# One-hots of the token ranks moved from VectorE to GpSimd, and their table products put one turn later

## The chip, the core and the metric

The kernel runs on one core of one Trainium2 chip. The metric is the device time of one launch in microseconds (us). The runs of the kernel before took 353.4, 355.7 and 352.9 us, a median of 353.4 us. One further execution was recorded by the hardware profiler; its own time is given below beside its span.

## What is computed

The reference first runs a gated linear attention over 4 batches, 8 heads, 768 positions and 48 features, with a complex decay for each feature. Then it sends each of the 3072 resulting rows to one of 8 experts.

```python
mag = np.sqrt(a_re * a_re + a_im * a_im)
scale = np.minimum(mag, 0.999) / (mag + 1e-06)
for t in range(S):
    S_re, S_im = (ar * S_re - ai * S_im + kv, ar * S_im + ai * S_re)
    y[:, :, t] = np.einsum('bhd,bhde->bhe', q[:, :, t], S_re)
...
logits = x @ w_gate + modality_bias[modality_id]
e_idx = np.argmax(logits, axis=1)
...
for e in range(E):
    h = np.maximum(x[mask] @ w1[e], 0.0)
    out[mask] = gate_w[mask, None] * (h @ w2[e])
```

## The kernel before, in words

**The attention part.** The 768 positions are cut into 6 chunks of 128; with 4 batches that makes 24 columns of 128 tokens. `gate_loop` walks over them in turns `w` from -4 to 24. Several stages are in flight in a turn: the decays of columns some turns ahead (angles `u`, waves `css`, moduli `pm`), the scaled queries and keys (`hats`, lines L276 and L280, which write `qkp` and `QK`), their transposes (`turned`, L304: `tKT` and `tQT`), the products within a column (`inner`: `wp` L321, the masked `W` L322, `up` L329, then `mid` L334, `U` L339, `state` L341), the output (`outer`: `yp` L353 and L359), and the rows with the logits (`rows`: `xw` L370, a copy `xr` L373 that is stored to `x_rows`, and the sum `lg` L374 on VectorE). Even turns also make the log sums `ls` L240, odd turns the angles `u` L194 and L195.

**The router.** `Router.take(m0, m1, ...)` is a generator that handles a group of columns in steps, one step for each turn. Four groups are taken: columns 0 to 8 from turn 8 on, 8 to 16 from turn 16 on, 16 to 20 from turn 20 on, and 20 to 24 after the last turn (`takes`). The first step picks each token's expert on VectorE. The second step counts, by products with a triangle of ones on TensorE, which rank a token has in its expert (`rank`), splits that position into its low 7 bits and the rest (`part` L654), and makes two one-hot matrices for each column: `lo` (128 tokens by 128, L658, the one-hot times the token's number) and `hi` (128 tokens by 194, L660, the one-hot times a power of two for the column), both bf16. The third step multiplies them on TensorE into a table (`table` L665), adds it to `so_far` on VectorE (L672), and after column 16 also runs `early_places` (some 30 small VectorE instructions from `counted` L688 to L690 on) and makes the index list `rows`, from which the first tokens can be gathered. Between its first and second step, gate weights `gw` (L619, L621) are worked out and stored to `x_rows` by small transfers on SyncE's queue (L624).

**The experts.** `Layers` loads two guessed experts' weights on GpSimd's queue (`w1` L863, `w2` L872) while the turns still run, issues gathers of token rows on GpSimd's queue (L913) from turn 22 on, once the first `rows` and `column` are there, transposes them (`xg_ps` L933), and runs two products per tile (`h_ps` L951, `y_ps` L966), whose results GpSimd's queue scatters (L971).

**What sets the order.** The Tile framework plans the order of each engine's instructions ahead of time, from the order of the program text, from when an instruction's inputs are there by its own costs, and from when a buffer comes free. On the chip each engine then goes through its list in that order. PSUM results share four slots (`pair`, tag "pair", bufs=4): `tKT`, `tQT`, `ls`, `wp`, `up`, `yp`, `xw`, `u`, `rank`, `cnt` and `table` take them in turn, and each waits until the reader of the one four places earlier is done. `lo` and `hi` have eight buffers each, `part` two. SyncE's queue (loads of `V` L285 and of q and k L138 and L139, stores of `x_rows`) and GpSimd's queue go in order too. [...]

Of the kernel before, what the change touches and what calls it, by code (L numbers as in the profile page):

```python
# [14 lines left out]
Alu = mybir.AluOpType  # L15
# [475 lines left out]
class Router:  # L491
# [88 lines left out]
    def take(self, m0, m1, late, dense):  # L580

        nc, rp, TP, E = self.nc, self.rp, self.TP, self.E
        n = m1 - m0
        last = m1 == len(self.tile_of)
# [68 lines left out]
        part = rp.tile([TP, 2, M], F32, name="part")  # L653
        nc.vector.tensor_copy(part[:, :, 0:n], part_i[:, :, 0:n])  # L654
        made = []
        for i in range(n):
            lo = rp.tile([TP, 128], BF16, name="lo", bufs=8)
            nc.vector.tensor_scalar(lo[:], self.iob[:, 0:128], part[:, 0, i:i + 1], self.p1[:], Alu.is_equal, Alu.mult)  # L658
            hi = rp.tile([TP, self.NC], BF16, name="hi", bufs=8)
            nc.vector.tensor_scalar(hi[:], self.iob[:, 0:self.NC], part[:, 1, i:i + 1], 2.0 ** self.tile_of[m0 + i], Alu.is_equal, Alu.mult)  # L660
            made.append((lo, hi))
        yield
        table = self.bank([128, self.NC], "table")
        for i, (lo, hi) in enumerate(made):
# [421 lines left out]
```

## Time and profile before

| | us |
|---|---|
| median of the runs | 353.4 |
| profiled execution, own time | 343.76 |
| its span in the trace | 341.9 |
| TensorE busy | 301.9 |
| VectorE busy | 256.0 |
| ScalarE busy | 241.2 |
| GpSimd busy | 70.0 |

The span is the time from the first to the last instruction of the trace. Busy time is the sum over instructions of an engine, overlaps counted once. On VectorE neighbouring instructions overlap by a little, so the distance between two starts says more about the cost of an instruction than its duration does. A bracket behind a row gives the idle time of the engine ahead of the instruction and what ended it. TensorE's attention turns lie between some 30 and 250 us; the experts' tiles follow until the end.

### The profile page before, as it was taken

Reading aid. Unit: us, or ns where it says so; the run is one execution under the profiler, and the core shown is the slowest. Engines: PE = TensorE matmul, PEld = TensorE weight load, DVE = VectorE, ACT = ScalarE, POOL = GpSimd, SP = SyncE. Lnnn points to the kernel's source line nnn. Section 1 sums busy time; section 2 is a strip of 40 time slices with the busy share of each in tenths; the row PEclk is TensorE's granted clock in tenths of the full one; section 3 lists DMA queues with packets and bytes.
Section 4 is the critical chain, followed back from the end, with each engine's and each line's share of the span. In section 5 each row is a group of like instructions: output and inputs, shape, how many; then the busy total and the mean of one; then the engine's idle time right before and its main releaser. Section 6 shows DMA issues by size and latency. Waiting matters only on the chain.

```text
span 341.9 us, 11679 instructions
## 1 busy us (share of the span) xinstructions
PE 301.9 (88%) x4982; PEld 232.8 (68%) x4982; DVE 256.0 (75%) x514; ACT 241.2 (71%) x301; POOL 70.0 (20%) x89
## 2 busy tenths in 40 slices
PE   1785999799989998999989999989999999979960
PEld 0342677577876878777777878789877687756740
DVE  2659799999895989999898889985679356543420
ACT  3888899999993999888898986445236554533530
POOL 8000000000000000001000001014202787887740
PEclk9999899899976999999999999999999999998995
DMA  7968788796777287864979794565110232322320
GB/s 144 219 117 164 154 182 161 115 188 136 134 179 131 63 141 168 148 142 67 160 176 181 149 166 80 86 87 117 39 38 18 81 111 83 104 92 92 113 90 4
DMA packets 158306, 41.21 MB, mean 121 GB/s; under 512 B 149107, under 2 KB 154632, under 8 KB 158250
## 3 DMA queue, kind: packets, MB, share of 16 engines
q1 hardware_dynamic: 152570, 30.08, 45.2%
q0 software_dynamic: 5680, 10.34, 12.5%
q8 instruction: 41, 0.67, 0.8%
q14 instruction: 15, 0.12, 0.1%
HBM read 36.39 MB, written 7.35 MB: 128 GB/s over the span
## 4 chain that ended last, share of the span: by engine, by line
PE 37%; ACT 21%; DVE 18%; DMA 9%; issue 8%; POOL 2%; SPq 2%; ACTq 0%; POOLq 0%; DVEq 0%
PE y_ps L966 6%; PE h_ps L951 6%; ACT sq L119 4%; PE up L329 4%; ACT L116 4%; PE yp L359 3%; PE xw L370 3%; PE u L194 3%; ACT css L119 3%; DMA qk<-in_k_dram 3%; DMA xg<-x_rows,idx 2%; PE wp L321 2%; ACT pm L119 2%; DMA abs<-in_a_re_dram 2%; DVE qkp L276 2%
## 5 line engine op out<-in xcount | busy, mean ns | idle before, releaser
L280 DVE TENSOR_TENSOR QK<-css,qkp 128x1536 f32<-128x1536 f32 x24 | 42.0, 1751 | 0.2
L329 PE MATMUL up<-V,QK 64*96 64x48 f32 x704 | 37.6, 248 | 2.4 <-DVE lg L374 2.4
L329 PEld LDWEIGHTS up<-V,QK 64*96 64x96 f32 x704 | 34.5, 162 | 4.2 <-DVE lg L374 2.8
L966 PE MATMUL y_ps<-w2t,hT 128*128 128x384 bf16 x200 | 36.8, 337 | 0.3 <-ACT hT L954 0.3
L971 POOL DMA_INDIRECT out_dram<-y_sb,idx x25 | 30.4, 1217 | 32.0 <-ACT y_sb L969 24.7
L863 POOL DMA_DIRECT2D abs<-in_moe_w_dram x2 | 1.8, 906 | 168.9 <-ACT sq L119 168.9
L951 PE MATMUL h_ps<-xgT,w1t 128*128 128x256 bf16 (+1 forms) x312 | 34.9, 268 | 0.0
L116 ACT ACT_TABLE_LOAD x25 | 32.1, 1283 | 1.4 <-PEq L1070 0.9
L951 PEld LDWEIGHTS <-w1t 128*128 128x128 bf16 x312 | 29.5, 98 | 4.6
L913 POOL DMA_INDIRECT xg<-x_rows,idx x25 | 28.8, 1153 | 14.5 <-issue 9.4
L305 ACT COPY KT<-tKT 96x1024 f32<-96x1024 f32 x24 | 24.2, 1006 | 10.2 <-PE tKT L304 10.2
L969 ACT ACTIVATE y_sb<-y_ps,xg 128x384 f32<-128x384 f32 x25 | 13.2, 577 | 24.8 <-PE y_ps L966 23.2
L321 PEld LDWEIGHTS wp<-QT,KT 96*64 96x64 f32 x768 | 24.3, 138 | 9.1 <-ACT yT L360 2.7
L321 PE MATMUL wp<-QT,KT 96*64 96x64 f32 x768 | 27.6, 225 | 2.9 <-ACT yT L360 2.0
L966 PEld LDWEIGHTS <-hT 128*128 128x128 bf16 x200 | 19.4, 101 | 13.5 <-issue 2.4
L370 PE MATMUL xw<-sel,yT 64*128 64x56 f32 x384 | 27.1, 283 | 0.7 <-ACT QT L305 0.7
L360 ACT COPY yT<-yp 128x512 f32<-128x512 f32 x24 | 14.0, 583 | 19.3 <-PE yp L359 19.2
L370 PEld LDWEIGHTS xw<-sel,yT 64*128 64x128 f32 x384 | 24.0, 193 | 2.6 <-ACT QT L305 0.8
L956 DVE TENSOR_SCALAR hT<-h_ps 128x1024 bf16<-128x1024 f32 (+1 forms) x10 | 11.7, 1171 | 18.4 <-PE h_ps L951 18.4
L194 PE MATMUL u<-tan,turn 128*128 128x384 f32 x48 | 23.3, 570 | 2.1 <-ACT tan L119 2.1
L305 ACT COPY QT<-tQT 96x1024 f32<-96x1024 f32 x24 | 24.3, 1013 | 0.8 <-PE tQT L304 0.7
L119 ACT ACTIVATE sq<-sq 128x1536 f32<-128x1536 f32 (+1 forms) x20 | 23.3, 1165 | 1.5 <-DVE sq L150 1.3
(209 smaller groups left out, 626.7 us busy)
## 6 DMA issues: line engine op xcount, KB each, us to landing
abs<-in_a_re_dram SPq DMA_DIRECT2D x24, 192.0 KB
abs<-in_a_im_dram SPq DMA_DIRECT2D x24, 192.0 KB
qk<-in_q_dram SPq DMA_DIRECT2D x24, 192.0 KB
qk<-in_k_dram SPq DMA_DIRECT2D x24, 192.0 KB
V<-in_v_dram SPq DMA_DIRECT2D x24, 192.0 KB
cb<-f_scr SPq DMA_DIRECT2D x10, 384.0 KB
x_rows<-xr SPq DMA_DIRECT2D x24, 96.0 KB
abs<-in_moe_w_dram POOLq DMA_DIRECT2D x2, 768.0 KB, 8.4
```

What stands on the lines that cost most here:

```text
L116: then(nc.scalar.preload_act_table_set(name))
L119: then(nc.scalar.activation(*args, **kw))
L194: nc.tensor.matmul(us[:, i], turn[:], tan[:, i], start=True, stop=False)
L280: nc.vector.tensor_tensor(QK[:].rearrange("p a h c d -> p a (h c d)"), wave, twice, Alu.mult)
L305: nc.scalar.copy(to[:], tp)
L321: nc.tensor.matmul(wp[rows_, h, :], KT[:, s, h], QT[:, s, h], start=True, stop=True)
L329: ins = nc.tensor.matmul(up[:, s, h], flat[rows_, h * C:(h + 1) * C], V[rows_, h, 0:D], start=True, stop=True)
L370: ins = nc.tensor.matmul(xw[:, u, j], yT[at_u, j], sel[at_u, j], start=True, stop=True)
L913: got = nc.gpsimd.indirect_dma_start(out=xg, out_offset=None, in_=self.x_rows, in_offset=bass.IndirectOffsetOnAxis(ap=idx[:, s, 0:1], axis=0))
L951: nc.tensor.matmul(h_ps[:, f // nf, f % nf, :], w1t[:, k, ff * 128:(ff + 1) * 128], xgT[:, k, :], start=(k == 0), stop=(k == KD - 1))
L966: nc.tensor.matmul(y_both[:, s], self.hT[:, f, s * 128:(s + 1) * 128], w2t[:, f, :], start=(f == 0), stop=(f == NF - 1))
L971: sc = nc.gpsimd.indirect_dma_start(out=self.out, out_offset=bass.IndirectOffsetOnAxis(ap=idx[:, s, 1:2], axis=0), in_=y_sb[:], in_offset= ...
```

## The change

In `Router.take`, the one-hots of the first three groups (20 columns, 40 instructions) go to GpSimd; the last group stays on VectorE. For the first three groups the generator also yields once more between the one-hots and the table products, so that the products and what follows them (`so_far`, and after column 16 `early_places` and the first `rows`) come in the turn after.

```diff
         made = []
         for i in range(n):
             lo = rp.tile([TP, 128], BF16, name="lo", bufs=8)
-            nc.vector.tensor_scalar(lo[:], self.iob[:, 0:128], part[:, 0, i:i + 1], self.p1[:], Alu.is_equal, Alu.mult)
+            eng = nc.vector if last else nc.gpsimd
+            eng.tensor_scalar(lo[:], self.iob[:, 0:128], part[:, 0, i:i + 1], self.p1[:], Alu.is_equal, Alu.mult)
             hi = rp.tile([TP, self.NC], BF16, name="hi", bufs=8)
-            nc.vector.tensor_scalar(hi[:], self.iob[:, 0:self.NC], part[:, 1, i:i + 1], 2.0 ** self.tile_of[m0 + i], Alu.is_equal, Alu.mult)
+            eng.tensor_scalar(hi[:], self.iob[:, 0:self.NC], part[:, 1, i:i + 1], 2.0 ** self.tile_of[m0 + i], Alu.is_equal, Alu.mult)
             made.append((lo, hi))
+        if not last:
+            yield
         yield
         table = self.bank([128, self.NC], "table")
```

## The prediction

> **What bounds the kernel now.** I read the page's busy times first, then the windows view for the turns in which the one-hots are made, then the chain of waits that ended last, then what TensorE waited for, and at last the instructions of each engine in order of time.
>
> ```profile
> PE 301.9 (88%) x4982; PEld 232.8 (68%) x4982; DVE 256.0 (75%) x514; ACT 241.2 (71%) x301; POOL 70.0 (20%) x89
> ```
> ```profile
> 142.40:151.50 9.10, 8.55 (x184) 6.96 (x184) 9.10 (x42) 7.24 (x9) 0.00 (x0) 1.00 0.74 166
> 151.50:160.00 8.50, 7.26 (x185) 6.59 (x185) 8.50 (x16) 8.10 (x10) 0.49 (x1) 1.00 0.13 17
> 212.00:230.00 18.00, 16.84 (x398) 14.67 (x398) 17.63 (x72) 8.20 (x12) 0.88 (x1) 1.00 0.61 88
> 230.00:236.00 6.00, 6.00 (x160) 5.67 (x160) 1.45 (x3) 3.50 (x8) 3.95 (x4) 1.00 0.84 155
> 242.00:248.00 6.00, 6.00 (x139) 5.41 (x137) 5.54 (x20) 0.82 (x2) 0.00 (x0) 1.00 0.14 38
> ```
>
> Behind the length of each window stand the busy times of TensorE, of its weight loads, of VectorE, ScalarE and GpSimd, then the clock granted to TensorE, the DMA share and GB/s. The averages of the page hide two states. Where the first two groups of one-hots are made (142 to 160 and 212 to 230 us), VectorE is full: 9.10 of 9.10, 8.50 of 8.50, 17.63 of 18.00. TensorE is nearly full beside it: 8.55, 7.26, 16.84. Where the third group is made (242 to 248), TensorE is full, 6.00 of 6.00. GpSimd does next to nothing in all of them. So there are two limits close together, and what VectorE is relieved of is worth only as much as TensorE stands still for VectorE.
>
> The chain of waits does run through the one-hots (start, us, what):
>
> ```profile
> 147.52 0.23 DVE lo L658
> ...
> 159.04 0.58 SPq L138
> 159.63 0.05 issue
> 159.68 9.29 DMA qk<-in_k_dram
> ```
>
> Read alone, this says that the one-hots lie on the path that sets the end. But the chain is one path of several that are about as long. The view of the waits of TensorE between 147 and 228 us (total, times, longest) says what it lost there:
>
> ```profile
> PE tQT L304 <- DVE eci L690: 1.2, 1, 1.2
> PE up L329 <- DVE lg L374: 1.0, 1, 1.0
> PE wp L321 <- DVE lg L374: 0.9, 1, 0.9
> PE wp L321 <- ACT yT L360: 0.7, 2, 0.4
> PE ls L240 <- DVE lg L374: 0.6, 1, 0.6
> PE tKT L304 <- DVE gw L621: 0.3, 1, 0.3
> ```
>
> The five on VectorE (DVE) make 4.0 us in 81. One of them, the 1.0 of `up`, I put down to the transfer of q and k (9.29 us in the chain), for which VectorE waits at that place. The other four, 1.2 + 0.9 + 0.6 + 0.3 = 3.0 us, are what TensorE loses to a VectorE that is late behind the one-hots.
>
> **The change part by part.**
>
> *VectorE is relieved.* Its rows around the first group (start, us):
>
> ```profile
> 147.45 0.30 DVE L658 TENSOR_SCALAR lo<-iob,part,p 128x128 bf16<-128x128 bf16 x1
> ...
> 150.43 0.29 DVE L658 TENSOR_SCALAR lo<-iob,part,p 128x128 bf16<-128x128 bf16 x1
> 150.65 0.26 DVE L660 TENSOR_SCALAR hi<-iob,part 128x194 bf16<-128x194 bf16 x1
> 150.83 0.67 DVE L322 TENSOR_TENSOR W<-wp,mask 128x512 f32<-128x512 f32 x1
> ```
>
> The durations, 0.29 and 0.26, would make 20 x 0.55 = 11 us. They overlap, though: eight pairs stand between 147.45 and the start of `W` at 150.83, so they cost 3.38 us, and one pair 0.42. Twenty pairs free 8.4 us of VectorE. What TensorE can make of it is at most the 3.0 us above; the third group gives nothing, since TensorE never waits there. SyncE's queue does not widen this: its load of q and k is issued at 159.04, behind TensorE's products of that turn in the chain, so it comes earlier only by what TensorE gains. Bounds of this gain: 0 and 3.0 us.
>
> *GpSimd is loaded.* No GpSimd row shows this instruction. The nearest are these three, one from the view of each source line (count, then min/median/max in ns):
>
> ```profile
> L48 POOL TENSOR_SCALAR_AFFINE_SELECT mask<-mask x1: 291/291/291, 2.6 to 2.6; 128x128 f32<-128x128 f32 x1
> L54 POOL TENSOR_SCALAR half<-mask x1: 544/544/544, 3.7 to 3.7; 128x128 f32<-128x128 f32 x1
> L559 POOL TENSOR_SCALAR_AFFINE_SELECT tri<-ones x1: 778/778/778, 7.6 to 7.6; 128x128 bf16<-128x128 bf16 x1
> ```
>
> The tensor-scalar of 128 elements takes 0.54 us; `hi` has 194, so scaled it is 0.82, and a pair 1.36. The low end is the select `mask` (0.29 and 0.44, a pair 0.73), the high end the bf16 select `tri` (0.78 and 1.18, a pair 1.96). I take 1.36, since it is the same kind of instruction. Eight pairs are 10.9 us (5.8 to 15.7), four pairs 5.4 us. The positions `part` are there at about 147 (the first `lo`), 214 and 243.8:
>
> ```profile
> 213.78 0.18 DVE part L654
> ```
> ```profile
> 243.58 0.17 DVE L654 CAST part<-part_i 128x8 f32<-128x8 int32 x1
> ```
>
> So undisturbed one-hots end at about 158, 225 and 249.2.
>
> *The products wait for them.* One turn later, they stand behind the angles `u` of the odd turn or behind its rows `xw`:
>
> ```profile
> 161.48 0.33 PE L195 MATMUL u<-neg,halfb 128*128 128x384 bf16 x1
> ```
> ```profile
> 227.95 1.10 PE L370 MATMUL xw<-sel,yT 64*128 64x56 f32 x16
> ...
> 249.70 2.00 PE L370 MATMUL xw<-sel,yT 64*128 64x56 f32 x32
> ```
>
> That is at 161.8 for the first group, at 229.0 for the second, and about 250.7, between the two halves of the last `xw` rows, for the third. The covers are 3.8, 4 and 1.5 us, less what TensorE gains: enough at 1.36 us a pair. At 1.96 a pair the one-hots end at 162.7, 229.7 and 251.6, so TensorE would wait 0.9 + 0.7 + 0.9 = 2.5 us. That is the price if the cover goes.
>
> *The two engines share something.* This speaks against the change, and the trace shows it at its start, where both run:
>
> ```profile
> 6.53 0.83 DVE L159 TENSOR_SCALAR neg<-abs 128x768 bf16<-128x768 f32 x1 [5.41 <-DMA abs<-in_a_re_dram]
> 7.29 0.94 DVE L157 TENSOR_TENSOR tan<-abs 128x768 f32<-128x768 f32 x1
> ```
> ```profile
> L159 DVE TENSOR_SCALAR neg<-abs x12: 544/550/835, 6.5 to 165.5; 128x768 bf16<-128x768 f32 x12
> ```
>
> The `neg` at 6.53 takes 0.83 us beside a working GpSimd, against a median of 0.55, so 0.28 more. The select `tri` on GpSimd (7.6 to 8.4) lies under VectorE's two-input `tan` (7.29 to 8.23) and takes 0.78; `mask`, made while VectorE is idle, takes 0.29, so 0.49 less. If every one of sixteen GpSimd instructions met a VectorE instruction in this way, VectorE would lose 16 x 0.28 = 4.5 us, more than the 3.38 it is spared, and GpSimd 16 x 0.49 = 7.8 us. The other end is no loss at all. Part of VectorE's work in these turns reads PSUM (`W`, `mid`, `U`), and neither row was taken with such work; I take six tenths, nearer to the two rows than to nothing. VectorE loses 2.7 of the 3.38 us, and GpSimd ends 4.7 us later for the big groups and, with less work beside it, some 1.2 us later for the small one: at about 162.6, 229.6 and 250.4. VectorE's net relief is then 0.7 us a group, so TensorE gains some 0.5 us at each of the first two groups (-1.0). It waits 0.8 and 0.6 us for the first two products, and 0.2 us more at each because it arrives earlier (+1.8).
>
> [...]
>
> *What else moves.* The load of w1 stands behind the first one-hots on GpSimd's queue, and the gathers near the third group's:
>
> ```profile
> 159.51 1.02 POOL L863 DMA_DIRECT2D abs<-in_moe_w_dram  x1 [151.13 <-ACT sq L119]
> ...
> 230.58 1.06 POOL L913 DMA_INDIRECT xg<-x_rows,idx  x1 [3.55 <-ACT idx L908]
> ```
>
> If the one-hots end at 162.6, w1 starts 3 us later than 159.51; what hides it are the turns up to 250, before whose end no product reads it. `early_places` and the first `rows` go one turn, some 6 us, later. VectorE has room there (1.45 busy of 6.00 from 230 on), so nothing is added; without that room it would be their some 30 small instructions. The first gather goes from 230.58 to about 237; six of them at 1.06 us and a gap end near 245, and their first use is a transpose behind the last `xw`, after 251.7 (249.70 and 2.00): hidden by 3 us and more after landing. They do share GpSimd's queue with the third group (5.4 us from 243.8 on) and can push its end from 250.4 to about 251.7, which costs 0 to 1.0 us of TensorE; I take 0.7. The `table` takes its PSUM slot one turn later. The wait of 1.2 us for `eci` is such a slot wait, on a small read that stands late in VectorE's list. It may go or come back double: -1.2 to +1.2, taken as 0, as neither row nor order tells.
>
> **Sum.** -1.0 + 1.8 + 0.7 + 0 = +1.5 us. Against the profiled execution's own 343.8 us that is 345.3. The runs shown have a median of 353.4, 9.6 us more than this one execution; I carry the difference over: 354.9 us, 0.4% more.
>
> **The rivals.**
>
> *GpSimd is starved, and TensorE waits for the products (slower).* The two-input instructions are the bulk of VectorE's turns (mean in ns behind the busy time):
>
> ```profile
> L280 DVE TENSOR_TENSOR QK<-css,qkp 128x1536 f32<-128x1536 f32 x24 | 42.0, 1751 | 0.2
> L276 DVE TENSOR_TENSOR qkp<-qk,pm 128x768 f32<-128x768 f32 x24 | 22.7, 948 | 1.0 <-DMA qk<-in_k_dram 0.9
> ```
>
> Two of each come in two turns, 2 x 1.75 + 2 x 0.95 = 5.4 us, and with a `tan` and a `sq` of 0.94 each 7.3 us. If GpSimd stands still during all of them, the first group ends at 147 + 10.9 + 7.3 = 165.2, 3.4 us behind the place of its product; the second, with 5.4 us beside it, at 214 + 10.9 + 5.4 = 230.3, 1.3 us behind. With 1.1 us lost net by VectorE at each big group (4.5 against 3.38) and 1.3 us at the third group, that is 3.4 + 1.3 + 2.2 + 1.3 = +8.2: 361.6 us, 2.3% more. It makes the kernel slower by over 1% as soon as the waits for the products exceed some 4 us together, that is from about 1.7 us a pair with 0.3 us lost by VectorE for each instruction. For it: VectorE is busy 8.50 of 8.50. Against it: some of its work reads PSUM, and the planner can put other products ahead.
>
> *VectorE's relief comes through whole (faster).* GpSimd goes undisturbed and all four waits go: -3.0, so 350.4 us, 0.8% less. To be faster by over 1% the wait of 1.0 at `up` must go too: 349.4 us. The 8.4 us of VectorE cannot come back, as TensorE is full.
>
> *The relief was hidden anyway.* TensorE's waits only change places, and GpSimd is in time: 353.4 us.
>
> **How the numbers follow.** About 1% (3.5 us) is what a measurement of this kernel can tell from no change. My sum (0.30), the case of no effect (0.12) and the faster case where it stays at -3.0 (0.08) make "within 1%" 0.50. The starved GpSimd, from over 1% on, has 0.40; faster by over 1% has 0.10. The range runs from 350.4, all four waits gone, to 361.6, the starved case in full; about one in ten lies outside at either side. The likeliest case alone has 351.9 to 356.9.
>
> **What would show it.** Right: one-hots on GpSimd at 1.3 to 2 us a pair; `QK`, `qkp` or `sq` beside them longer than 1.75 and 0.95; the waits of 0.9, 0.6 and 0.3 smaller; table products that wait about 1 us; the first gather near 237. Wrong: table products with waits of several us or one-hots of over 2 us a pair (the starved case); VectorE's instructions unstretched and none of the four waits left (the faster one). A new order of the planner, with waits at places not named here, would make the whole working miss.

## The result, and the profile after

| | before | after |
|---|---|---|
| median of the runs, us | 353.2 (6 runs, 342.6 to 355.7) | 374.8 (6 runs, 369.9 to 381.4) |
| ratio, 95% interval | | 1.0848 (1.0778 to 1.0918) |
| profiled execution, us (span) | 343.76 (341.9) | 375.1 (373.1) |
| its mean granted clock | 0.959 | 0.924 |

The change makes the kernel 8% slower. The ratio leaves disturbed executions out, so it is larger than the quotient of the medians. The prediction was 354.9 us, its range 350.4 to 361.6.

The page of the kernel after, first the busy times, then the granted clock in 40 slices, then the two groups that the change moved (count, busy time, mean ns of one, idle time before):

```profile
PE 314.3 (84%) x4982; PEld 238.5 (64%) x4982; DVE 249.4 (67%) x474; ACT 240.9 (65%) x301; POOL 114.8 (31%) x129
...
PEclk9989899899999999979999999695969996999995
...
L659 POOL TENSOR_SCALAR lo<-iob,part,p 128x128 bf16<-128x128 bf16 x20 | 20.7, 1033 | 145.3 <-DVE part L654 144.6
...
L280 DVE TENSOR_TENSOR QK<-css,qkp 128x1536 f32<-128x1536 f32 x24 | 42.2, 1757 | 0.2
...
L661 POOL TENSOR_SCALAR hi<-iob,part 128x194 bf16<-128x194 bf16 x20 | 28.6, 1432 | 0.8
```

A pair of one-hots costs GpSimd 1.03 + 1.43 = 2.47 us on average, where the prediction took 1.36 and a high end of 1.96. `QK` on VectorE takes 1757 ns against 1751: VectorE is not stretched.

What TensorE waited for in the kernel after:

```profile
PE table L668 <- POOL hi L661: 14.6, 11, 1.6
...
PE y_ps L969 <- issue: 4.4, 2, 3.4
...
PE wp L321 <- issue: 2.4, 4, 1.1
```

The first row is new: eleven waits, 14.6 us. The waits on VectorE that the prediction counted on (`eci` 1.2, `ls` 0.6, `gw` 0.3, the 0.9 of `wp`) are gone, but around the first group others have come in their place (0.4 for ScalarE's `yT`, 0.6 of `up` for VectorE). The two rows with "issue" name nothing that the trace shows; they come back below.

GpSimd in order of time, first group:

```profile
144.17 1.52 POOL L659 TENSOR_SCALAR lo<-iob,part,p 128x128 bf16<-128x128 bf16 x1 [135.63 <-DVE part L654]
...
148.48 4.77 POOL L661 TENSOR_SCALAR hi<-iob,part 128x194 bf16<-128x194 bf16 x1
153.24 1.76 POOL L659 TENSOR_SCALAR lo<-iob,part,p 128x128 bf16<-128x128 bf16 x1
...
162.51 0.79 POOL L659 TENSOR_SCALAR lo<-iob,part,p 128x128 bf16<-128x128 bf16 x1
163.29 0.94 POOL L661 TENSOR_SCALAR hi<-iob,part 128x194 bf16<-128x194 bf16 x1
164.21 0.79 POOL L659 TENSOR_SCALAR lo<-iob,part,p 128x128 bf16<-128x128 bf16 x1
165.10 0.95 POOL L661 TENSOR_SCALAR hi<-iob,part 128x194 bf16<-128x194 bf16 x1
```

VectorE over the slow `hi`:

```profile
148.83 0.94 DVE L176 TENSOR_TENSOR tan<-tan,sq 128x768 f32<-128x768 f32 x1
149.69 1.74 DVE L280 TENSOR_TENSOR QK<-css,qkp 128x1536 f32<-128x1536 f32 x1
151.36 0.21 DVE L374 TENSOR_REDUCE lg<-xw 128x8 f32<-128x64 f32 x1
151.50 0.94 DVE L276 TENSOR_TENSOR qkp<-qk,pm 128x768 f32<-128x768 f32 x1
152.47 1.87 DVE L280 TENSOR_TENSOR QK<-css,qkp 128x1536 f32<-128x1536 f32 x1
```

The group runs from 144.17 to 166.05, 21.9 us. An undisturbed `hi` takes 0.94 us; the one at 148.48 takes 4.77: it begins before `tan`, stands through `tan`, `QK` and `qkp`, and ends in the second `QK`. All four read two inputs. VectorE pays 0.13 us at most (the second `QK`, 1.87 against 1.74). So the two engines do share something, but the loss lies on GpSimd: 3.83 us in this one `hi`.

TensorE at the first group's products:

```profile
157.52 0.41 PE L668 MATMUL table<-hi,lo 128*128 128x194 bf16 x3
159.00 0.24 PE L668 MATMUL table<-hi,lo 128*128 128x194 bf16 x1 [1.06 <-POOL hi L661]
...
166.09 0.32 PE L668 MATMUL table<-hi,lo 128*128 128x194 bf16 x1 [1.50 <-POOL hi L661]
166.35 1.09 PE L304 MATMUL tKT<-ident,QK 64*96 64x64 f32 x16
```

The eight products stand in one block in TensorE's order, directly behind `u`. From the fourth on, TensorE waits for each of them at GpSimd's pace, and what stands behind them comes only with the last (`tKT` at 166.35). The block takes 166.41 - 157.52 = 8.9 us. Then `tKT` takes 1.09 us where 0.65 was usual: the clock has fallen. The windows of the kernel after around its waits (the columns as in the prediction; the granted clock stands third from the end):

```profile
157.00:162.80 5.80, 1.65 (x9) 0.66 (x7) 2.40 (x4) 0.97 (x3) 5.61 (x7) 1.00 0.90 150
162.80:169.60 6.80, 3.85 (x37) 2.59 (x37) 2.91 (x5) 1.92 (x2) 4.15 (x5) 0.50 0.49 93
169.60:175.00 5.40, 5.40 (x135) 4.46 (x133) 3.08 (x6) 4.14 (x5) 0.00 (x0) 1.00 0.97 189
...
234.50:241.30 6.80, 4.20 (x65) 3.67 (x67) 3.34 (x24) 1.92 (x2) 3.75 (x5) 0.50 0.38 42
...
251.60:261.80 10.20, 10.20 (x126) 8.63 (x127) 2.24 (x9) 1.42 (x3) 1.90 (x2) 0.50 0.13 31
```

TensorE works 1.65 of 5.80 us from 157 on, and half the clock follows for 6.8 us; the second block of products does the same at 234.5. No single wait here lasts over 1.63 us; what went ahead was a stretch thinly filled. Half clock also came behind one much fuller. The profile of the kernel before has it behind two waits of 0.42 and 0.72 us that end at 97.3:

```profile
98.60:108.80 10.20, 10.20 (x122) 7.70 (x122) 6.35 (x10) 5.43 (x7) 0.00 (x0) 0.50 0.84 152
```

There TensorE had worked 3.46 of the 4.60 us ahead (94.0 to 98.6). The same two waits, 0.42 and 0.72 us, at 134 to 136 us of that profile, with the same 3.46 of 4.60 us worked (132.9 to 137.5), left the clock at 1.00.

The longest stretch of the kernel after in its turns, from 251.6 on, comes behind something else. TensorE at turn 22, in the midst of one run of `wp`:

```profile
246.54 0.89 PE L321 MATMUL wp<-QT,KT 96*64 96x64 f32 x9
247.87 0.34 PE L321 MATMUL wp<-QT,KT 96*64 96x64 f32 x4 [0.44 <-issue]
248.63 0.34 PE L321 MATMUL wp<-QT,KT 96*64 96x64 f32 x4 [0.42 <-issue]
249.37 0.37 PE L321 MATMUL wp<-QT,KT 96*64 96x64 f32 x5 [0.41 <-issue]
250.84 0.55 PE L321 MATMUL wp<-QT,KT 96*64 96x64 f32 x10 [1.10 <-issue]
...
256.78 1.96 PE L370 MATMUL xw<-sel,yT 64*128 64x56 f32 x16
```

No instruction of this run waits for another engine, yet TensorE gets only four matmuls through in 0.75 us. From this `wp` to the end of `xw` it takes 12.2 us; the kernel before takes 5.3 for the same (its `wp` at 236.02, its `xw` at 240.24 and 1.10). GpSimd issues the first gathers at just that time:

```profile
245.01 1.07 POOL L916 DMA_INDIRECT xg<-x_rows,idx  x1 [6.77 <-ACT idx L911]
246.39 0.99 POOL L916 DMA_INDIRECT xg<-x_rows,idx  x1 [0.30 <-issue]
247.68 0.95 POOL L916 DMA_INDIRECT xg<-x_rows,idx  x1 [0.30 <-issue]
248.94 0.95 POOL L916 DMA_INDIRECT xg<-x_rows,idx  x1 [0.30 <-issue]
```

Where the 31 us between the two profiled spans arise can be read from the starts of the same instructions in both (us):

| TensorE's instruction | before | after | after is later by |
|---|---|---|---|
| first `u` ahead of the first block of products | 159.93 | 155.81 | -4.1 |
| `tKT` behind that block | 161.74 | 166.35 | 4.6 |
| `xw` ahead of the second block | 227.95 | 230.15 | 2.2 |
| `tKT` behind it | 228.88 | 237.78 | 8.9 |
| the `wp` with the stand | 236.02 | 246.54 | 10.5 |
| `rank` behind its `xw` | 241.28 | 258.68 | 17.4 |
| first `xg_ps` of the experts | 251.63 | 274.34 | 22.7 |
| end of the span | 341.9 | 373.1 | 31.2 |

The first two blocks cost 8.7 and 6.7 us, of which 7.1 and 4.9 are waits for GpSimd. The stand at the gathers and the half clock behind it cost 6.9. The 5.3 between `rank` and `xg_ps` hold the third block, with 2.5 of waits, and more half clock. The last 8.5 come in the experts, where TensorE stands again with "issue" (the 4.4 us of `y_ps`) and half clock follows. This last part does not belong to the change alone: the run below that moves the outer groups has the time of the kernel before, and its profile shows 4.8 us of the same wait of `y_ps`.

### The profile page after: what moved, and what is told of

The parts are those of the page before. It is cut to its first block, busy times and chain, and to the rows that moved or that the text cites. A ratio compares the mean times of both kernels' runs of the same rounds, so it can differ in the third digit from the quotient of the medians.

```text
span 373.1 us, 11686 instructions
## 1 busy us (share of the span) xinstructions
PE 314.3 (84%) x4982; PEld 238.5 (64%) x4982; DVE 249.4 (67%) x474; ACT 240.9 (65%) x301; POOL 114.8 (31%) x129
## 4 chain that ended last, share of the span: by engine, by line
PE 34%; POOL 8%; issue 8%; DVE 2%; DMA 1%; ACT 1%; POOLq 0%; ACTq 0%; DVEq 0%
PE h_ps L954 4%; PE up L329 4%; PE y_ps L969 4%; PE xw L370 4%; PE wp L321 3%; PE yp L359 3%; POOL hi L661 3%; POOL out_dram L974 2%; POOL lo L659 2%; PE yp L353 2%; PE ls L240 2%; PE tKT L304 2%; POOL xg L916 2%; PE rank L92 1%; PE tQT L304 1%
## 5 line engine op out<-in xcount | busy, mean ns | idle before, releaser
L659 POOL TENSOR_SCALAR lo<-iob,part,p 128x128 bf16<-128x128 bf16 x20 | 20.7, 1033 | 145.3 <-DVE part L654 144.6
L969 PE MATMUL y_ps<-w2t,hT 128*128 128x384 bf16 x200 | 38.2, 342 | 6.6 <-issue 4.4
L280 DVE TENSOR_TENSOR QK<-css,qkp 128x1536 f32<-128x1536 f32 x24 | 42.2, 1757 | 0.2
L329 PE MATMUL up<-V,QK 64*96 64x48 f32 x704 | 38.5, 249 | 2.3 <-DVE lg L374 2.3
L974 POOL DMA_INDIRECT out_dram<-y_sb,idx x25 | 26.9, 1077 | 37.1 <-ACT y_sb L972 30.5
L329 PEld LDWEIGHTS up<-V,QK 64*96 64x96 f32 x704 | 35.5, 164 | 4.2 <-DVE lg L374 2.8
L321 PE MATMUL wp<-QT,KT 96*64 96x64 f32 x768 | 30.1, 232 | 4.5 <-issue 2.4
L321 PEld LDWEIGHTS wp<-QT,KT 96*64 96x64 f32 x768 | 26.2, 144 | 11.2 <-issue 5.0
L661 POOL TENSOR_SCALAR hi<-iob,part 128x194 bf16<-128x194 bf16 x20 | 28.6, 1432 | 0.8
L370 PE MATMUL xw<-sel,yT 64*128 64x56 f32 x384 | 28.2, 289 | 0.6 <-ACT QT L305 0.6
L972 ACT ACTIVATE y_sb<-y_ps,xg 128x384 f32<-128x384 f32 x25 | 13.2, 579 | 21.9 <-PE y_ps L969 17.4
L370 PEld LDWEIGHTS xw<-sel,yT 64*128 64x128 f32 x384 | 24.9, 199 | 3.6 <-issue 1.1
```

Of the source, the lines that this page charges most:

```text
L280: nc.vector.tensor_tensor(QK[:].rearrange("p a h c d -> p a (h c d)"), wave, twice, Alu.mult)
L321: nc.tensor.matmul(wp[rows_, h, :], KT[:, s, h], QT[:, s, h], start=True, stop=True)
L329: ins = nc.tensor.matmul(up[:, s, h], flat[rows_, h * C:(h + 1) * C], V[rows_, h, 0:D], start=True, stop=True)
L370: ins = nc.tensor.matmul(xw[:, u, j], yT[at_u, j], sel[at_u, j], start=True, stop=True)
L659: eng.tensor_scalar(lo[:], self.iob[:, 0:128], part[:, 0, i:i + 1], self.p1[:], Alu.is_equal, Alu.mult)
L661: eng.tensor_scalar(hi[:], self.iob[:, 0:self.NC], part[:, 1, i:i + 1], 2.0 ** self.tile_of[m0 + i], Alu.is_equal, Alu.mult)
```

## The experiments

The expectations name three theories. A: the cost is TensorE's wait for GpSimd's one-hots. B: GpSimd stretches VectorE's instructions. C: moving the second group's products, and with them the early index and the gathers, costs by itself. Each set of runs has the kernel before beside it on the same chip; its median went from 338 to 352 us between these sessions, so a run is read against the ones beside it.

**Place and engine apart** (kernel before beside them: 347.1 us).

One more turn for the products (`if not last: yield; yield` in place of one `yield`):

> The changed kernel with one turn more between the one-hots on GpSimd and their products (two turns later than before). Theory A (TensorE stands still for one-hots that GpSimd has not finished, and its clock falls behind the stand): GpSimd still needs 19 to 22 us for a group of eight, which now ends about when the product is reached, so the waits of the products fall from 14.6 us in all to under 3 us, and the kernel comes within 1.5% of the one before (348 to 358 us). [...]

Measured 353.2 us, ratio 1.0226 (1.0095 to 1.0358). The waits for GpSimd are gone from the list of waits, and with them most of the loss. What is left, 2.3%, is more than the 1.5% that A allows. Its profile shows a stand with "issue" at 240 to 246 us with 17 us of half clock behind it.

The new place alone, with `eng = nc.vector` for all:

> The changed kernel with the one-hots back on VectorE: only the products stay one turn later. Theory A and theory B: within 1% of the kernel before (350 to 357 us), with no wait of a product over 0.5 us. Theory C (moving the products itself is what costs, through the PSUM slots, the first index list and the gathers that come a turn later): over 2% slower than before (360 us and more).

Measured 372.6, 362.2, 362.3 and 346.4 us, too spread for a ratio. In the slowest, which was the profiled one, TensorE has the same stand in the same `wp`, and half clock from 245 to 276. So the place can cost without GpSimd, but not in every execution; these four do not settle it.

GpSimd alone: the kernel before, plus unread copies of the one-hots on GpSimd (`lo2`, `hi2`, one buffer each). It adds work and leaves nothing out:

> The kernel before, in which GpSimd makes a second set of the 20 columns' one-hots that nothing reads; the output is untouched. It shows what GpSimd's work costs its neighbours when no product waits for it. Theory A: within 1% of the kernel before (350 to 357 us), VectorE's two-input instructions at 1.75 and 0.95 us as before, GpSimd's own stretched. Theory B: over 2% slower (360 us and more), with longer two-input instructions.

Measured 356.8 us, ratio 1.0357 (1.0246 to 1.0468). This missed for A. The time is as B expected, but B's sign, longer instructions on VectorE, is not there; its page says

```profile
L280 DVE TENSOR_TENSOR QK<-css,qkp 128x1536 f32<-128x1536 f32 x24 | 42.1, 1755 | 0.2
```

as before. B is out: GpSimd's one-hots did not stretch VectorE's instructions here (`QK` 1755 ns against 1751). Why this kernel lost 3.6% was not found. Its one profile has half clock that begins 12 us ahead of the first gather (232.45), behind a wait of 1.55 us of `tQT` for VectorE's `eci`, with TensorE busy throughout:

```profile
220.50:234.10 13.60, 13.60 (x204) 12.84 (x206) 6.80 (x34) 4.37 (x8) 12.61 (x13) 0.50 0.21 34
```

In the profile of the kernel before, the same wait is 1.16 us and the clock stays at 1.00.

The changed kernel with 36, 24 and 12 filler products on TensorE ahead of the three blocks (`dense({0: 36, 8: 24, 16: 12}[m0])`):

> The changed kernel with 36, 24 and 12 filler products (0.24 us each) ahead of the three groups' table products, in the bank that the table then overwrites; they take the place of the stand. Theory A: the stand itself stays (the last one-hot ends when it ends), but TensorE's clock does not fall behind it, so the products after it take 0.65 instead of 1.09 us (tKT): 3 to 10 us less than the changed kernel, 364 to 371 us. If the clock fall costs nothing or has another cause than the stand, the time stays at 372 to 378 us.

Measured 371.7 us (363.0 to 380.0), between the two expectations: no clear gain. The fillers take the place of the waits (1.2 us of them are left) and the clock no longer falls behind the blocks, but the stand at turn 22 and 27 us of half clock behind it stay. That the half clock behind the blocks is the smaller part of the loss is argued from this, not shown: the four runs are too spread.

**One group at a time** (kernel before: 346.7 us; for the third group 347.9).

The second group's products alone one turn later, all one-hots on VectorE:

```diff
+        if m0 == 8:
+            yield
         yield
```

> The kernel before, with VectorE making all one-hots; the products of columns 8 to 15 alone, and with them the early index and the first gathers, come one turn later. Theory C (the moved middle group costs by itself): TensorE stands some 2.5 us at turn 22 near the first gathers, half clock follows for 15 us or more, the experts' stand returns, and most runs lie 2 to 6% above the kernel before, time x mean granted clock staying near before's 335 us. Theory A (only waits for GpSimd's one-hots cost): within 1%, granted clock as before.

Measured 358.8 us, ratio 1.0302 (1.0214 to 1.039). The first and third group moved in the same way (`if m0 in (0, 16): yield`):

> The kernel before, with VectorE making all one-hots; the products of columns 0 to 7 and 16 to 19 come one turn later, those of 8 to 15 and the early index stay. Theory C: no stand at turn 22, within 1%. Theory A: within 1% too. If it is over 2% slower at a lower clock, then any shift of the products disturbs the clock, and the early index is not the cause.

Measured 345.4 us, ratio 1.0003 (0.9948 to 1.0059). Beside the same runs of the kernel before, this is the clean pair for C: the same edit, on the second group 3%, on the others nothing. The second group's run does no more work (time x mean granted clock is 333 to 338 us in its runs, 332 to 341 before); all it loses is clock. Its windows:

```profile
217.00:231.00 14.00, 13.55 (x253) 12.38 (x255) 8.56 (x39) 3.54 (x7) 0.88 (x1) 0.76 0.57 88
231.00:242.00 11.00, 8.79 (x142) 7.60 (x142) 3.22 (x13) 3.40 (x7) 4.89 (x5) 0.78 0.21 47
242.00:262.00 20.00, 20.00 (x263) 17.47 (x259) 8.41 (x24) 2.71 (x5) 0.94 (x1) 0.50 0.07 21
```

In the kernel before, the clock is 1.00 in all three.

The first group alone on GpSimd, one turn later as in the change:

> GpSimd makes the one-hots of columns 0 to 7 alone and their products come one turn later, as in the changed kernel; the other groups as before. Theory A: TensorE waits some 8 us for the eight products at 158 to 166 us and a short half clock adds 1 us, so the time is 8 to 9 us (2.5%) over before; with time x mean granted clock near 343 us. Theory C: the same, and no stand at turn 22. If it is 15 us or more over, the first group's wait carries the later clock falls as well.

Measured 352.5 us, ratio 1.0211 (1.0161 to 1.0261), some 7.3 us. Its waits:

```profile
PE table L668 <- POOL hi L661: 6.9, 5, 1.6
```

No stand over 0.5 us at turn 22. A holds here with its size. The same group two turns later (two more `yield`):

> GpSimd makes the one-hots of columns 0 to 7 alone, and their products come two turns later than before; everything else as before. Theory A: no wait of TensorE for GpSimd is left, VectorE is relieved of 16 one-hots, and the time is 0 to 1% under before. Theory B (GpSimd stretches VectorE's instructions): 1 to 2% over. Theory C: as A, since the early index stays where it was.

Measured 346.5 us, ratio 1.0039 (0.9979 to 1.0098). There is still one wait of 4.3 us, which A did not expect, since a `lo` was held up for 3.8 us, and yet the time is that of before; so VectorE's relief may pay for this wait, and not for more (argued from the two numbers, not tried).

The third group alone on GpSimd, one turn later:

> GpSimd makes the one-hots of columns 16 to 19 alone, their products come one turn later; the other groups as before. Theory A: GpSimd starts them after the gathers' issues, TensorE waits 2 to 4 us for the products, half clock follows for 3 to 7 us, 1 to 1.5% over before. If the gathers leave GpSimd free in time: no wait, within 1%. Theory C: no stand at turn 22 either way.

Measured 352.7 us, ratio 1.0137 (1.0015 to 1.0258), with 3.4 us of waits: this fits A's size too, though the interval is wide.

**The stand at the gathers.** In ScalarE's order the three index copies `idx`, each with a register load, had moved directly ahead of `KT`. C1 blames them; the edit gives them to VectorE (`engines=[ET.DVE ...]`, `nc.vector.tensor_copy`). With the second group moved, with the whole change, and with the kernel before (kernel before: 347.9 us):

> As the run that moves the second group alone, but the three index copies of the first gathers, each with its register load, are made by VectorE instead of ScalarE; the gathers go out at the same point. Theory C1 (the stand at turn 22 belongs to the three index loads that now stand in ScalarE's order right ahead of its copies KT and QT): no stand of TensorE in wp, no idle of some 2 us before KT, half clock after 215 us falls from 40 us to under 10, time within 1% of before. Theory C2 (it belongs to the gathers or to something else that lies there, whoever copies the indices): the stand and 30 us of half clock stay, 2 to 5% over before.

> The changed kernel, with the three index copies of the first gathers on VectorE. Theory C1: the stand at turn 22 and the half clock behind it go, 7 to 10 us under the changed kernel, 362 to 367 us; the waits for GpSimd's one-hots stay at 14 to 15 us. Theory C2: as the changed kernel, 370 to 378 us.

> The kernel before, with the three index copies of the first gathers on VectorE: the control. Both theories: within 1% of before, since the kernel before shows no stand there; if it shows a stand or loses 2% or more, the copy itself disturbs and the other two runs can't be read simply.

Measured 1.0315 (1.0187 to 1.0442), 1.0913 (1.0813 to 1.1012) and, the control, 1.0159 (1.0046 to 1.0272). C1 falls: with the second group moved, the stand stays (2.6 us of "issue" in `wp`). In the whole change 0.8 us of it is left, and 11.8 us of waits for one-hots, yet the time does not improve. The control showed more: now the kernel before has the stand too, in another instruction (`yp`, 231.4 to 234.7), and its gathers, of which four go out without a gap from 229.05 on, end at 233.9. In all eight kernels with this stand by then it began some 2 to 5 us after the first gather of a run without gaps, and ended about 1 us after the last (in the changed kernel 2.4 and 0.95 us, in this control 2.4 and 0.8). That gave theory D: gathers back to back hold up TensorE's instructions. (Against it stood from the start the profile of the kernel before, with four gathers in a row, 230.58 to 235.47, and no stand.) The edit puts GpSimd memsets between them:

```diff
+        if n in (1, 2):
+            for k in range(3):
+                nc.gpsimd.memset(both[:], k)
         for s in range(2 if i < self.big else 1):
```

(`n == 1` alone in the second run.) With the second group moved; with the products two turns later; with the whole change (kernel before: 351.8 us):

> As the run that moves the second group alone, with three GpSimd memsets between the gathers of one tile and those of the next, so that no more than two gathers go out back to back. Theory D (four gathers back to back hold up TensorE's instructions some 2 us after the first, until 0.9 us after the fourth; the moved group lets them go out so): no stand of TensorE in wp, half clock after 215 us falls from 41 us to under 10, time within 1% of before. Theory D2 (the place in the order counts, not the burst): the stand and 20 us or more of half clock stay, 2 to 4% over.

> The changed kernel with the products two turns later than before, and with three GpSimd memsets between the first two gathers and the next two. Theories A and D together: no wait for GpSimd's one-hots and no stand at the gathers, so within 1% of before. Theory D2: as without the memsets, 2% over.

> The changed kernel with three GpSimd memsets between the gathers of one tile and of the next. Theories A and D: the 14 to 15 us of waits for the one-hots stay, the stand at turn 22 and the 10 us of half clock behind it go: 7 to 10 us under the changed kernel, 362 to 368 us. Theory D2: as the changed kernel, 370 to 378 us.

Measured 0.998 (0.983 to 1.013), 1.0035 (0.996 to 1.011) and 1.0484 (1.0367 to 1.0601; 366.5 us). The same three kernels without memsets had 1.030, 1.023 and 1.085. The profiles show only two to four gaps of TensorE there, of up to 0.45 us, though in the profile of the first of the three 27 us of half clock still follow. TensorE in the changed kernel with memsets:

```profile
248.96 0.88 PE L321 MATMUL wp<-QT,KT 96*64 96x64 f32 x9
250.27 0.93 PE L321 MATMUL wp<-QT,KT 96*64 96x64 f32 x23 [0.43 <-issue]
```

Its wait for one-hots stays (14.2 us), as A says. The last two runs, side by side on one chip, are the cleanest measure of A: both make the one-hots on GpSimd, and one more turn for the products takes 366.5 us to 349.3. (One wait of 4.3 us is left in the second, where A expected none; its early index comes a turn later too, and it has memsets in one place instead of two.) These were other sessions than those without memsets, so the pair was run once more side by side, with the memsets in the kernel before as a control (kernel before: 338.4 us):

> The kernel before with three GpSimd memsets between the gathers of one tile and of the next: the control for the memsets. Theory D: the profile of before shows no stand at the gathers, so nothing is to be gained there: within 1% of before, at most 1% faster if some of its executions have the stand. If it is 2% faster, the spacing helps for a reason other than the moved group.

> The run that moves the second group alone, once more, to stand on the same chip beside the next one. Theory D: 2 to 4% over before, a stand of TensorE that begins some 2 us after the first of four gathers and ends 0.8 to 0.9 us after the fourth.

> The moved second group with the gathers spaced, once more, beside the run without the spacing. Theory D: 2% or more under that run and within 1% of before; no TensorE stand over 1 us at the gathers. Theory D2: as that run.

Measured 1.001 (0.9967 to 1.0052), 1.0038 (0.9996 to 1.0081) and 1.0001 (0.9953 to 1.005). The repeat of the moved group, which had lost 3%, lost nothing, though its gathers went out without a gap, six in a row:

```profile
229.19 1.06 POOL L916 DMA_INDIRECT xg<-x_rows,idx  x1 [7.66 <-ACT idx L911]
...
235.61 0.95 POOL L916 DMA_INDIRECT xg<-x_rows,idx  x1 [0.30 <-issue]
```

with TensorE under them at full clock and with full busy time:

```profile
231.00:242.00 11.00, 11.00 (x249) 9.85 (x246) 7.53 (x29) 2.74 (x6) 4.34 (x5) 1.00 0.34 74
```

So D is at best half of it: where the stand came, there was a run of gathers without gaps, but such a run also stands without it, here and in the profile of the kernel before. That spacing weakens the stand is not shown, since no kernel without memsets but with the group moved ran beside the spaced ones in a session that had the stand. Something outside the kernel decides whether it comes. This was the chip of the first four experiments, on which the stand had come; in the second one no profile showed it, in the turns or in the experts, and the kernel before was 9 us faster than in the first. What it is was not found, and the whole change was not tried in such a session.

**Half clock without the stand.** The two profiles of the kernel that moves the second group show one thing more. Where it cost 3%, it has half clock ahead of its first gather (231.17) as well, behind a wait of 0.63 us:

```profile
217.45 1.55 PE L329 MATMUL up<-V,QK 64*96 64x48 f32 x16 [0.63 <-DVE lg L374]
```
```profile
220.10:226.90 6.80, 6.80 (x90) 6.02 (x87) 2.68 (x19) 2.39 (x4) 0.85 (x1) 0.50 1.03 156
```

The repeat, the same kernel, has the same wait and keeps its clock:

```profile
218.04 1.55 PE L329 MATMUL up<-V,QK 64*96 64x48 f32 x16 [0.63 <-DVE lg L374]
```
```profile
217.00:231.00 14.00, 13.37 (x335) 12.38 (x333) 9.88 (x44) 6.13 (x12) 2.39 (x3) 1.00 0.59 90
```

So the same kernel with the same wait lost its clock in one execution and kept it in another, ahead of all gathers. How much of the 3% the stand caused, and how much such a fall, is not shown. Nor did full work bring the clock back soon: in the first of these executions, behind the stand, TensorE was busy 30.70 of 30.70 us at 0.50 (237.2 to 267.9).

## Why the prediction was wrong

*VectorE is relieved.* The size was near, the reason in the main another. TensorE came to the first products 4.1 us earlier than in the profile before, of which 2.9 lay ahead of the change. Of the other 1.2, some 0.8 is the block of products itself (0.83 us), which stood ahead of `u` before and now stands behind it; the prediction did not count this, and it shortens the cover. The waits there went only from 0.3 + 0.9 to 0.4 + 0.6 us. At the second group the 1.2 us for `eci` went, which the prediction took as 0. The rival "comes through whole" (-3.0) is not borne out: with the first group relieved and its products two turns later the time was 1.0039 of before, with one wait of 4.3 us left.

*GpSimd is loaded.* This term was mis-sized. The pair was taken at 1.36 us from the f32 tensor-scalar of 128 elements (`half`), with 1.96 from the bf16 select as the high end. Undisturbed it is 1.70 from start to start (162.51 to 164.21). Eight are 13.6 us and not 10.9. The bf16 row, nearer in type, was the better one.

*The two engines share something.* Right that they do, wrong in who pays. VectorE was to lose 2.7 us a group and lost 0.13 an instruction at most; GpSimd was to be 4.7 us late and was 21.9 - 13.6 = 8.3 in the first group, and 5.1 in the second (218.71 to 237.37). The row read as a stretched VectorE (`neg`, 0.83 against 0.55) did not carry over; in the profile after, the same `neg` beside the same GpSimd work takes 0.64. What the trace shows is a `hi` that took 4.77 us instead of 0.94 beside four two-input VectorE instructions (148.83 to 154.34), while none of the four took more than 0.13 us longer. The starved rival's 7.3 and 5.4 us, a GpSimd that stands still through all of `QK`, `qkp`, `tan` and `sq`, were the author's estimate; measured are the 8.3 and 5.1.

*The products wait for them.* This is the step that failed most. The sum had 0.8 + 0.6 + 0.4 us of waits and 0.7 for the third group, 2.5 in all; measured are 7.1, 4.9 and 2.5, which make the 14.6. The starved rival named the mechanism, and its chance of 0.40 was fair, but its price of 8.2 us held only 6.0 of such waits; with 1.70 us a pair it would have had 2.7, 2.7 and 1.4 us more, 12.8 of waits. For the third group the prediction took its 0.7 from gathers ahead of the one-hots; they had ended 5.4 us before the first one-hot (262.26), and GpSimd's pace alone made the wait. And the eight products stand in one block: TensorE did nothing else from 157.52 to 166.35.

*The clock.* The prediction took TensorE's clock as given, a term put at nothing without a reason. Its five windows showed 1.00, but the page it read has 0.7 and 0.6 in two slices (the 98.60 to 108.80 above). Behind the three blocks TensorE did 3.85, 4.20 and 6.70 us of work at half clock, which at full clock takes little more than half (an `xw` 1.10 us instead of 1.96); as an estimate from these windows that adds up to 7 us, and more behind the stand.

*What else moves.* "The first gather goes to about 237" and "nothing is added" failed: it went to 245.01. Moving the early index and the gathers cost 3% by itself in one session and 0.4% in another. The place of a stand of TensorE next to the gathers could not be read from the profile before, which has four gathers in a row (230.58 to 235.47) and no stand.

*The carried difference.* The sum was made against an execution of 343.8 us and shifted by 9.6 us to the median. The kernel before later ran at 338 to 352 us from session to session, so this shift was a guess as large as the effects counted.

What is settled: 14.6 us of waits for GpSimd's one-hots, and that the greater part of the loss goes with them (with the products one turn later still, 0 to 4.3 us of waits are left, and the time is 1.0226 and 1.0035 of before). The second group's move cost apart from them in one session and not in another. What stays open is what lets the clock fall in one execution and not in another, and what makes TensorE's instructions come at four matmuls in 0.75 us while gathers go out. The page of the kernel before shows DMA packets of the kind "instruction" (queue 8, 41 of them, 0.67 MB). Whether they have to do with the stand was not shown: of the three in the kernel after between 240 and 260 us one, at 249.1, lies under the stand.

## What to carry to other kernels

Before work goes to GpSimd, put its price at the slowest row of the same type, add the whole length of VectorE's two-input instructions that will run beside it (here 7.3 us by the prediction, and GpSimd was 8.3 late), and ask where the reader stands in TensorE's order: the first block here, which waited for each of its inputs, lost 7.1 us by it, and half clock followed for 6.8. A part of a change that "only moves" an index or a transfer needs a run of its own, and so does the same kernel in another session: here one moved `yield` cost 3% or nothing.

## What the runs showed of the hardware

- GpSimd's bf16 compare-and-multiply, undisturbed: 0.79 us for 128 elements, 0.94 for 194. VectorE does the pair in 0.42.
- Under back-to-back two-input VectorE work one such instruction took up to 4.77 us, while VectorE's took 0.13 more at most.
- TensorE's clock halved for 6.8 us behind waits of at most 1.63 us each, when TensorE had worked 1.65 of 5.80 us, and for 10.2 us behind waits of 0.42 and 0.72 us. Behind the same wait of 0.63 us it halved in one execution and stayed full in another.
- At half clock, 30.70 us of full work (30.70 of 30.70) did not raise it.
- While GpSimd issued gathers without a gap, TensorE issued four matmuls in 0.75 us in some sessions and went on undisturbed, 11.00 busy of 11.00, in another.
